# Reordering the first item of a fused block-sorted attention and gated MoE kernel, and issuing the later items' attention steps in pairs

## The chip, the cores and the metric

The kernel runs on one core of one Trainium2 chip. The metric is the device time of one execution in microseconds. Each comparison runs the kernel before and the variant in turn on the same chip, and a run of a single core is called slow when it is more than 1.5% above the fastest of the same kernel. Beside the time, each run records the length of its span and the mean clock that was granted to TensorE, as a share of full speed.

Four moments serve throughout as milestones, all read from TensorE's timeline: the **first scores** (first matmul into s_ps), the **second half of item 0** (the 33rd h matmul, the first for the second half of that item's tokens), the first h matmul of items 1, 2 and 3, and the end of TensorE. Everything ahead of the second half of item 0 is called the **front**.

## The reference

```python
for _ in range(5):                        # sinkhorn on (4, 8, 8, 8)
    P = exp(P - max(P, -1)); P = P / (sum(P, -1) + 1e-9); P = P / (sum(P, -2) + 1e-9)
k_sorted = einsum('bhij,bhjcd->bhicd', P, k_b)    # 8 blocks of 96 tokens, head_dim 64
v_sorted = einsum('bhij,bhjcd->bhicd', P, v_b)
attn = softmax(q_b @ k_sorted_b.T / 8)            # block i of q against sorted block i
x = (attn @ v_sorted_b) -> (3072, 512)            # batch 4, 8 heads, 768 tokens
out = maximum(x @ w1, x @ w2) @ w_out             # d_ff 1024
```

The kernel uses relu(x(w1 - w2)) + x w2 for the maximum, and multiplies w2 by w_out beforehand, so h is one product of 128x384 tiles and the output sums two.

## The kernel before

The four batch items follow one another. Item b's matmuls of h and of the output run while item b+1's attention steps are put between them. Only item 0's attention has nothing to hide behind. Dense zero matmuls, the fills, keep TensorE running while the sinkhorn iterations wait for VectorE.

```python
load_v(0, 0, 3); load_k(0); load_q(0)             # then weights, in order
...
keep_streaming(ps_f32("fill_ps"), 76 * 160, most=160)
for it in range(5):
    sinkhorn(it)            # at it 3 and 4: 3072 columns of fills behind the exponent
    ...                     # ScalarE turns the values in pieces
SC, VA, TR = att(0)         # steps: 8 scores, 8 values, 4 transpositions of x
sort_k(0, 0, 2048, "A"); sort_k(0, 1, 256, "D"); sort_k(0, 2, 256, "A")   # fills ahead of each
sort_v(0, 0, 0, "D"); sort_v(0, 1, 0, "A")
q_transposes(0, 0, "D")     # two head pairs
sort_v(0, 2, 0, "A"); scores(0, 0); sort_v(0, 3, 0, "D"); scores(0, 1)
q_transposes(0, 1, "D"); values(0, 0); ...
```

The letters say which engine empties the PSUM tile: A is ScalarE, D is VectorE. The kernel keeps four PSUM tiles of 128x1024 fp32.

The softmax here doesn't subtract the row's maximum and nothing guards it: scores larger than these inputs give would overflow.

Of the kernel before, what the change touches and what calls it, by code (L numbers as in the profile page):

```python
# [16 lines left out]
def kernel(  # L17
# [97 lines left out]
    kT = {}  # L115
# [62 lines left out]
    make_identity(nc, ident)  # L178
    load_k(0)
    load_q(0)  # L180
    load_w_columns(w2_sb, moe_w2, 0, 2)
    load_w_columns(w1_sb, moe_w1, 0, 1)
    load_w_columns(w1_sb, moe_w1, 1, 2)
# [3 lines left out]
    load_v(1)  # L187
# [12 lines left out]
    w_difference(0, nc.gpsimd)  # L200
    load_k(1)
# [24 lines left out]
    def sinkhorn(it):  # L226
        nc.scalar.activation(out=p_sb, in_=p_sb, func=AF.Exp)
        if it >= 3:
            late_zeros(it)
            keep_streaming(ps_f32("fill_ps"), 3072, it)  # L230
        nc.vector.reduce_sum(out=rowsum, in_=p_sb, axis=AX.X)
        nc.vector.reciprocal(out=rowsum, in_=rowsum)
        nc.vector.tensor_tensor(
            out=p_sb, in0=p_sb, in1=rowsum.to_broadcast([G, NB, NB]), op=ALU.mult
        )
        nc.vector.reduce_sum(out=colsum, in_=p_sb.transpose([0, 2, 1]), axis=AX.X)
        nc.vector.reciprocal(out=colsum, in_=colsum)
        nc.vector.tensor_tensor(
            out=p_bf if it == 4 else p_sb,
            in0=p_sb,  # L240
            in1=colsum.to_broadcast([G, NB, NB]).transpose([0, 2, 1]),
            op=ALU.mult,
        )
# [42 lines left out]
    def block_diagonals(b):  # L286

        pe = ps_f32("pe")
        kinds = [1] if b % 2 else [1, 0]
        for m in kinds:  # L290
            sel = (
                sel_k[b].rearrange("g h w -> g (h w)")
                if m
                else sel_v[b].rearrange("g h j -> g (h j)")
            )
            nc.tensor.matmul(
                pe[:, m * 64 : m * 64 + 64],
                sel,
                p_bf.rearrange("p i j -> p (i j)"),
                start=True,  # L300
                stop=True,
            )
        for m in kinds:
            pm = const.tile([128, NB, NB], FP32, tag=f"pm{m}", name="pm")
            nc.vector.tensor_tensor(
                out=pm,
                in0=pe[:, m * 64 : m * 64 + 64].rearrange("p (i j) -> p i j", j=NB),
                in1=maskJ[:, m].to_broadcast([128, NB, NB]).transpose([0, 2, 1]),
                op=ALU.mult,
            )  # L310
            pt = const.tile([128, NB], FP32, tag=f"pt{m}", name="pt")
            nc.vector.reduce_sum(out=pt, in_=pm, axis=AX.X)
            bd = const.tile([128, 8, NB], BF16, tag=f"bd{m}{b}", name="bd")
            nc.vector.tensor_tensor(
                out=bd,
                in0=maskM[:, m].to_broadcast([128, 8, NB]),
                in1=pt.to_broadcast([128, NB, 8]).transpose([0, 2, 1]),
                op=ALU.mult,
            )
            if m:  # L320
                bd_k[b] = bd.rearrange("p m i -> p (m i)")
            else:
                bd_v[b] = bd_v[b + 1] = bd.rearrange("p m i -> p (m i)")
# [18 lines left out]
    def q_transposes(b, half, eng=None):  # L342

        if half == 0:
            qT[b] = qpool.tile([128, HP, R, 128], BF16, tag="qT", name="qT")
        if b > 1:
            hps = slice(half * 2, half * 2 + 2)
# [6 lines left out]
        for n in range(2 * R):  # L354
            hp, r = half * 2 + n // R, n % R
            c = slice(n * 128, (n + 1) * 128)
            for h2 in range(2):
                nc.tensor.matmul(  # L358
                    ps[h2 * 64 : h2 * 64 + 64, c],
                    q_raw[b][:, hp + 4 * h2, r * D : (r + 1) * D],  # L360
# [6 lines left out]
            qT[b][:, half * 2 : half * 2 + 2].rearrange("p h r c -> p (h r c)"),  # L367
            ps[:, 0 : 2 * R * 128],
            2 * R * 128,
# [4 lines left out]
    def sort_k(b, t, n=0, eng=None):  # L374
# [4 lines left out]
        for c in range(16):  # L379
# [10 lines left out]
        evac(  # L390
            kT[b][:, 0 : 32 * BLK]
            .rearrange("p (m ch c) -> p ch m c", ch=2, m=32)[:, :, :, t * 16 : (t + 1) * 16],
            ps.rearrange("p (c ch m) -> p ch m c", ch=2, m=32),
            1024,
            eng=eng,
        )

    def sort_v(b, t, n=0, eng=None):
# [3 lines left out]
        for m in range(16):  # L402
# [10 lines left out]
            ps[0:BLK].rearrange("p (d m) -> p m d", m=64),  # L413
            1024,
# [246 lines left out]
    keep_streaming(ps_f32("fill_ps"), 76 * 160, most=160)  # L661
    for it in range(5):
        sinkhorn(it)
# [4 lines left out]
        if it == 2:  # L668
            selections(0)
            turn_v(first, "A", 0, 18)  # L670
        if it == 3:
            turn_v(first, "A", 18, 36)
    turn_v(first, "A", 36, 56)
    turn_v(first, "A", 56, 80)
    block_diagonals(0)
    turn_v(first, "D", 80, 96)

    SC, VA, TR = att(0)
    sort_k(0, 0, 2048, "A")
    sort_k(0, 1, 256, "D")  # L680
    sort_k(0, 2, 256, "A")
    sort_v(0, 0, 0, "D")
    sort_v(0, 1, 0, "A")
    q_transposes(0, 0, "D")
    sort_v(0, 2, 0, "A")
    scores(0, 0)
    sort_v(0, 3, 0, "D")
    scores(0, 1)
    q_transposes(0, 1, "D")
    values(0, 0)  # L690
# [3 lines left out]
    values(0, 2, 256)  # L694
    x_transposes(0, 0, "A")
    VA[3]()
    SC[4]()
    moe_h_products(0, 0, 0, (0, 2), 256)
    x_transposes(0, 1, "A")
    w_difference(1)  # L700
    moe_h_products(0, 0, 1, (0, 2))
    for b in range(1, B):
        selections(b)
    w_difference(2)
    w2_out = w2_transposes(0, "D")
    moe_h(0, 0, 0, "A", (1, 3))
    w2_out()
    w_difference(3)
    moe_h(0, 0, 1, "A", (1, 3))
    SC[5]()  # L710
# [5 lines left out]
    def load_rest():  # L716
# [4 lines left out]
        0: [VA[4]],  # L721
        1: [SC[6], SC[7], VA[5]],
        2: [VA[6], TR[2], VA[7]],
        3: [TR[3], lambda: w2_transposes(1, "A")(), load_rest, lambda: block_diagonals(1)],
# [8 lines left out]
    for b in range(B):  # L733
# [15 lines left out]
        if b == B - 1:  # L749
            units += [  # L750
                lambda: moe_out_last(4, [(0, 512, "D")]),
                lambda: moe_out_last(5, [(0, 256, "A"), (256, 384, "D"), (384, 512, "A")]),
            ]
        steps, lo = [], 2
        if b < B - 1:
            qs = [lambda half=half: q_transposes(b + 1, half) for half in range(2)]
# [6 lines left out]
            if b == 0:  # L763
                lo = 9
                tail[7] += ks
# [3 lines left out]
                steps = group(*vs[:3]) + qs[:1] + group(*SC[0:2], vs[3]) + qs[1:] + VA[:1]  # L769
                steps += group(*SC[2:5]) + VA[1:2]  # L770
            elif b == 1:
                vs = [lambda t=t: sort_v_pair(2, t) for t in range(8)]
                tail[1] = qs
                tail[10] = [lambda: pair_q(3, 0), lambda: pair_q(3, 1)]
                steps = group(*ks) + group(*vs[0:3]) + group(*vs[3:6]) + group(*vs[6:8])
                steps += group(*SC[0:2]) + group(*SC[2:4]) + VA[:2]
            else:
                tail[1] = qs
                tail[4] = ks
                steps = group(*SC[0:2]) + group(*SC[2:5]) + VA[:2]  # L780
                lo = 6
            rest = SC[4:] if b == 1 else SC[5:]
            steps += VA[2:3] + TR[:1] + VA[3:4]
            steps += group(*rest[:-1]) + TR[1:2] + VA[4:5] + rest[-1:] + VA[5:6]
            steps += TR[2:3] + VA[6:7]
# [10 lines left out]
        tail = {0: [VA[7], TR[3]]}  # L796
# [28 lines left out]
```

## Time and profile before

| | value |
|---|---|
| median (range) of the first three runs | 178.76 us (177.56 to 180.59) |
| profiled span, clock | 175.0 us, 0.998 |
| first scores | 18.53 us |
| second half of item 0 | 35.66 us |
| first h of items 1, 2, 3 | 74.22, 110.55, 144.31 us |
| end of TensorE, of the span | 171.6, 175.0 us |

These lines are of the kernel before. On the page below, each digit of a row is the busy share, or the clock, of one of 40 equal slices in tenths; a queue row gives packets, MB and share.

```profile
span 175.0 us, 4519 instructions
...
PEclk9999999999999999999999999999999999999999
...
q8 instruction: 16, 0.26, 0.6%
```

The row of queue 8 is easily skipped. It says that a DMA queue moved 16 packets of instructions, 0.26 MB or 16 KB each, while the kernel ran. TensorE's timeline: start, busy time, operation, count, and in brackets the idle time before it with what ended it. In all these lines PE is TensorE, PEld its weight loads, DVE VectorE, ACT ScalarE and POOL GpSimd; L82 is a line of the kernel.

```profile
9.43 2.54 PE L82 MATMUL fill_ps<-fill,late 128*128 128x512 bf16 x11
...
12.05 1.04 PE L82 MATMUL k_ps<-fill 128*128 128x512 bf16 x4
...
13.65 0.28 PE L82 MATMUL k_ps<-fill 128*128 128x256 bf16 x1
```

Fills stand in every gap from 1.2 to 14.5 us, and no bracket appears between them.

### The profile page before, as it was taken

Reading aid. Unit: us, or ns where it says so; the run is one execution under the profiler, and the core shown is the slowest. Engines: PE = TensorE matmul, PEld = TensorE weight load, DVE = VectorE, ACT = ScalarE, POOL = GpSimd, SP = SyncE. Lnnn points to the kernel's source line nnn. Section 1 sums busy time; section 2 is a strip of 40 time slices with the busy share of each in tenths; the row PEclk is TensorE's granted clock in tenths of the full one; section 3 lists DMA queues with packets and bytes.
Section 4 is the critical chain, followed back from the end, with each engine's and each line's share of the span. In section 5 each row is a group of like instructions: output and inputs, shape, how many; then the busy total and the mean of one; then the engine's idle time right before and its main releaser. Section 6 shows DMA issues by size and latency. Waiting matters only on the chain.

```text
span 175.0 us, 4519 instructions
## 1 busy us (share of the span) xinstructions
PE 162.3 (93%) x1999; PEld 99.8 (57%) x2014; DVE 83.1 (47%) x186; ACT 79.9 (46%) x98; POOL 22.9 (13%) x39
## 2 busy tenths in 40 slices
PE   7999799999999899997999899999798999899992
PEld 7948666756665454466665445566454446454461
DVE  5867797559355737225638324235254442221110
ACT  4576576797253454069880622436803106330030
POOL 7951453122302002000000000000000000000000
PEclk9999999999999999999999999999999999999999
DMA  4999999999999952999201245292024154400333
GB/s 59 200 206 204 202 209 214 206 202 208 220 209 205 196 151 51 117 245 270 64 0 22 87 104 156 104 208 48 0 48 140 27 165 142 26 0 0 120 123 120
DMA packets 29811, 23.11 MB, mean 132 GB/s; under 512 B 16672, under 2 KB 24736, under 8 KB 29792
## 3 DMA queue, kind: packets, MB, share of 16 engines
q0 software_dynamic: 10304, 12.58, 42.5%
q1 hardware_dynamic: 19200, 10.04, 23.6%
q8 instruction: 16, 0.26, 0.6%
q10 hardware_dynamic: 288, 0.20, 0.3%
q14 instruction: 3, 0.02, 0.0%
HBM read 25.17 MB, written 6.29 MB: 180 GB/s over the span
## 4 chain that ended last, share of the span: by engine, by line
PE 73%; DMA 9%; ACT 6%; issue 5%; DVE 2%; POOL 2%; ACTq 0%; DVEq 0%; POOLq 0%
PE out_ps L612 33%; PE h_ps L585 23%; DMA q_raw<-in_q_dram 7%; PE wc_ps L563 4%; PE o_ps L477 3%; PE k_ps L383 3%; ACT e L458 3%; PE s_ps L450 2%; DMA xT<-x 2%; ACT g L599 2%; PE tq_ps L358 1%; PE v_ps L404 1%; DVE qT L106 1%; PE tw_ps L540 1%; POOL k_raw L145 1%
## 5 line engine op out<-in xcount | busy, mean ns | idle before, releaser
L612 PE MATMUL out_ps<-wo_sb,g 128*128 128x512 bf16 (+2 forms) x198 | 46.2, 362 | 1.8 <-DVE o L106 0.7
L585 PE MATMUL h_ps<-xT,w_sb 128*128 128x384 bf16 x256 | 45.2, 326 | 1.9 <-DMA xT<-x 0.8
L585 PEld LDWEIGHTS <-w_sb 128*128 128x128 bf16 x256 | 24.1, 98 | 17.4 <-issue 2.3
L458 ACT ACTIVATE e<-s_ps 96x768 bf16<-96x768 f32 x32 | 24.0, 807 | 19.4 <-PE s_ps L450 19.4
L612 PEld LDWEIGHTS <-g 128*128 128x128 bf16 x208 | 18.0, 97 | 17.5 <-issue 1.2
L599 ACT ACTIVATE g<-h_ps 128x768 bf16<-128x768 f32 x23 | 18.6, 812 | 18.1 <-PE h_ps L585 18.1
L612 PE MATMUL out_ps<-wc,xT 128*128 128x512 bf16 (+2 forms) x103 | 24.8, 362 | 0.1
L104 ACT COPY o<-out_ps 128x1024 f32<-128x1024 f32 x8 | 8.1, 1012 | 35.7 <-PE out_ps L612 29.4
L494 DVE TENSOR_TENSOR x<-o_ps,rs 96x512 bf16<-96x512 f32 x32 | 22.0, 687 | 1.1
L488 DVE RECIPROCAL rs<-o_ps 96x8 f32<-96x8 f32 x32 | 6.4, 201 | 32.2 <-PE o_ps L477 32.2
L601 DVE TENSOR_SCALAR g<-h_ps 128x768 bf16<-128x768 f32 x9 | 8.6, 957 | 18.2 <-PE h_ps L585 18.2
L612 PEld LDWEIGHTS <-xT 128*128 128x128 bf16 x104 | 9.9, 98 | 10.9
L477 PEld LDWEIGHTS <-e 96*128 96x128 bf16 x256 | 11.7, 97 | 7.0 <-issue 0.9
L477 PE MATMUL o_ps<-v_sb,e 96*128 96x65 bf16 x256 | 13.1, 193 | 1.4 <-ACT e L458 1.0
L106 DVE CAST v_sb<-v_ps 96x1024 bf16<-96x1024 f32 x8 | 9.7, 1217 | 8.0 <-PE v_ps L425 5.1
L450 PE MATMUL s_ps<-qT,kT 64*128 64x96 bf16 x256 | 9.2, 204 | 1.6 <-DVE qT L106 0.9
L104 ACT CAST kT<-k_ps 128x1024 bf16<-128x1024 f32 x9 | 8.8, 1016 | 3.0 <-PE k_ps L383 3.0
L450 PEld LDWEIGHTS <-kT 64*128 64x128 bf16 x256 | 6.3, 94 | 6.6 <-issue 4.8
L104 ACT CAST v_sb<-v_ps 96x1024 bf16<-96x1024 f32 x8 | 7.9, 1012 | 3.8 <-PE v_ps L404 3.7
L82 PEld LDWEIGHTS <-fill 128*128 128x128 bf16 x84 | 8.7, 123 | 1.7 <-DVE fill L73 1.2
L82 PE MATMUL fill_ps<-fill 128*128 128x160 bf16 x76 | 8.2, 292 | 1.2 <-DVE fill L73 1.2
L106 DVE COPY o<-out_ps 128x1024 f32<-128x1024 f32 x3 | 3.7, 1225 | 9.3 <-PE out_ps L612 9.3
(73 smaller groups left out, 132.5 us busy)
## 6 DMA issues: line engine op xcount, KB each, us to landing
out_dram<-o SPq DMA_DIRECT2D x11, 512.0 KB, 3.0
k_raw<-in_k_dram POOLq DMA_DIRECT2D x12, 256.0 KB, 12.4
q_raw<-in_q_dram POOLq DMA_DIRECT2D x4, 768.0 KB, 10.8
v_raw<-in_v_dram POOLq DMA_DIRECT2D x6, 384.0 KB, 12.7
w_sb<-in_moe_w_dram POOLq DMA_DIRECT2D x3, 512.0 KB, 16.0
wo_sb<-in_moe_w_out_dram POOLq DMA_DIRECT2D x2, 512.0 KB, 19.9
v_raw<-in_v_dram POOLq DMA_DIRECT2D x3, 256.0 KB, 4.6
w_sb<-in_moe_w_dram POOLq DMA_DIRECT2D x2, 256.0 KB, 14.1
```

The source lines that it names most:

```text
L82: nc.tensor.matmul(ps[:, 0:w], w0, fill[:, 0:w], start=True, stop=True)
L104: nc.scalar.copy(out=out_ap, in_=in_ap)
L106: nc.vector.tensor_copy(out=out_ap, in_=in_ap)
L450: nc.tensor.matmul(ps[:, h2 * 512 + ii * 128 : h2 * 512 + ii * 128 + BLK], kT[b][rows, (hp * 8 + i) * BLK : (hp * 8 + i) * BLK + 128], rhs ...
L458: nc.scalar.activation(out=e[:, 0 : 8 * BLK].rearrange("p (t c r) -> p t c r", t=8, r=R), in_=ps[0:BLK] .rearrange("p (t f) -> p t f", t=8 ...
L477: nc.tensor.matmul(ps[:, h2 * 512 + ii * 65 : h2 * 512 + (ii + 1) * 65], e[:, (h2 * 4 + ii) * BLK : (h2 * 4 + ii) * BLK + 128], v_sb[:, m0 ...
L494: nc.vector.tensor_tensor(out=x, in0=ov[:, :, :, 0:D], in1=rs.to_broadcast([BLK, 2, 4, D]), op=ALU.mult,)
L563: nc.tensor.matmul(wc_ps[0][:, m * 512 : (m + 1) * 512], w2T[:, fb, dmt * 128 : (dmt + 1) * 128], wo_sb[:, fb, :], start=(fb == 0), stop=( ...
L585: nc.tensor.matmul(h_ps[t][:, m * 512 : m * 512 + TCH], w1_sb[:, hp, fb * 128 : (fb + 1) * 128], xT[:, b % 2, ch, hp % 2, hp // 2, :], sta ...
L599: nc.scalar.activation(out=g, in_=src, func=AF.Relu)
L601: nc.vector.tensor_scalar(out=g, in0=src, scalar1=0.0, scalar2=None, op0=ALU.max)
L612: nc.tensor.matmul(dst, g_tiles[b, ch, m // 2][:, m % 2, off : off + 128] if m < NFB else xT[:, b % 2, ch, hp % 2, hp // 2, off : off + 12 ...
```

## The change

The intent: let the scores start from one head pair of queries, let values of the first four blocks be ready early, take the fills out where real work can stand, and issue the later attention steps in pairs so that four PSUM tiles have time to empty.

```diff
+    load_q(0)
     load_k(0)
-    load_q(0)
-    load_w_columns(w2_sb, moe_w2, 0, 2)
-    load_w_columns(w1_sb, moe_w1, 0, 1)
-    load_w_columns(w1_sb, moe_w1, 1, 2)
+    for w in range(2):
+        load_w_columns(w2_sb, moe_w2, w, w + 1)
+        load_w_columns(w1_sb, moe_w1, w, w + 1)
...
-    def sinkhorn(it):
+    def sinkhorn(it, meanwhile=None):
         nc.scalar.activation(out=p_sb, in_=p_sb, func=AF.Exp)
-        if it >= 3:
+        if meanwhile:
+            meanwhile()                     # VectorE turns 11 columns of values
+        if it == 4:
             late_zeros(it)
-            keep_streaming(ps_f32("fill_ps"), 3072, it)
+            keep_streaming(ps_f32("fill_ps"), 2048, it)
...
-    keep_streaming(ps_f32("fill_ps"), 76 * 160, most=160)
+    keep_streaming(ps_f32("fill_ps"), 174 * 72, most=72)
...
-    sort_k(0, 0, 2048, "A")
-    sort_k(0, 1, 256, "D")
-    sort_k(0, 2, 256, "A")
-    sort_v(0, 0, 0, "D")
-    sort_v(0, 1, 0, "A")
-    q_transposes(0, 0, "D")
-    sort_v(0, 2, 0, "A")
-    scores(0, 0)
+    q_transposes(0, 0, 1, "A")              # one head pair
+    sort_v_half(0, 0, 0, "D")               # first four blocks, 32 columns
+    sort_v_half(0, 0, 1, "A")
+    sort_k(0, 0, 0, "D")
+    sort_k(0, 1, 0, "A")
+    sort_k(0, 2, 0, "AD")                   # emptied in two halves
+    SC[0]()
... (item 0's remaining steps, with the second half sorts between values 1 to 3)
-                lambda: moe_out_last(5, [(0, 256, "A"), (256, 384, "D"), (384, 512, "A")]),
+                lambda: moe_out_last(5, [(0, 384, "D"), (384, 512, "A")]),
...
-            steps += VA[2:3] + TR[:1] + VA[3:4]
-            steps += group(*rest[:-1]) + TR[1:2] + VA[4:5] + rest[-1:] + VA[5:6]
-            steps += TR[2:3] + VA[6:7]
+            steps += group(*SC[0:2]) + VA[0:1] + group(*SC[2:4]) + VA[1:2] + group(VA[2], TR[0])
+            steps += group(*SC[4:6]) + VA[3:4] + group(VA[4], TR[1]) + group(*SC[6:8]) + VA[5:6]
+            steps += group(VA[6], TR[2]) + VA[7:8] + TR[3:4]
...
-        tail = {0: [VA[7], TR[3]]}
+        tail = {}
```

## The prediction

The spacing of 31 ns in its later stages is that of 48 value matmuls in 1.50 us, at 46.73 us of the trace before, and the 0.17 us of a free array are the author's estimate from it and from the page's mean of 193 ns (L477). Its rate of 205 GB/s is from the GB/s row of the profile's page (207 from 4.4 to 61 us). That VectorE works off its queue in the order of the program was assumed for the walk; the waits for x (1.14, 1.46 and 1.56 us, walked as 1.2, 1.7 and 1.7) agree with it.

> **What bounds the kernel now.** I read the page first, then the chain of waits in order of time, then the timeline of each engine with the idle time in brackets.
>
> ```profile
> PE 162.3 (93%) x1999; PEld 99.8 (57%) x2014; DVE 83.1 (47%) x186; ACT 79.9 (46%) x98; POOL 22.9 (13%) x39
> ```
>
> TensorE is the bound on average, the other engines are half empty. So only two things can shorten the kernel: fewer TensorE instructions on the path, or less time in which TensorE stands still. The chain says where it starts, and the timeline where it stands still:
>
> ```profile
> 5.09 11.48 DMA q_raw<-in_q_dram
> 16.57 0.04 issue
> 16.61 0.88 PE tq_ps L358 x24
> ```
> ```profile
> 18.53 0.35 PE L450 MATMUL s_ps<-qT,kT 64*128 64x96 bf16 x8 [0.48 <-DVE qT L106]
> ...
> 20.63 0.40 PE L477 MATMUL o_ps<-v_sb,e 96*128 96x65 bf16 x8 [0.35 <-DVE v_sb L106]
> ...
> 57.57 0.40 PE L477 MATMUL o_ps<-v_sb,e 96*128 96x65 bf16 x8 [0.62 <-ACT e L458]
> ...
> 81.30 0.41 PE L425 MATMUL v_ps<-bd,v_dc 64*128 64x64 bf16 x16 [0.51 <-ACT kT L104]
> ...
> 82.22 1.46 PE L585 MATMUL h_ps<-xT,w_sb 128*128 128x384 bf16 x8 [0.51 <-ACT kT L104]
> ...
> 99.08 1.89 PE L612 MATMUL out_ps<-wo_sb,g 128*128 128x512 bf16 x7 [0.53 <-ACT o L104]
> ...
> 123.39 0.35 PE L450 MATMUL s_ps<-qT,kT 64*128 64x96 bf16 x8 [0.35 <-ACT e L458]
> ...
> 124.09 1.46 PE L585 MATMUL h_ps<-xT,w_sb 128*128 128x384 bf16 x8 [0.35 <-ACT e L458]
> ...
> 132.84 1.89 PE L612 MATMUL out_ps<-wo_sb,g 128*128 128x512 bf16 x7 [0.68 <-DVE o L106]
> ...
> 151.01 5.04 PE L585 MATMUL h_ps<-xT,w_sb 128*128 128x384 bf16 x30 [0.76 <-DMA xT<-x]
> ```
>
> The reader is to see three regions. Until 16.6 us the inputs arrive (values, keys, queries, in that order, and the queries last). From 18.5 to about 35 us the first item's attention runs with little other work beside it. After that TensorE is nearly full, and its stops are short waits for a PSUM tile that ScalarE or VectorE has not emptied yet (three score tiles issued in a row, three key tiles and three value tiles in a row), and one wait for a transpose by DMA.
>
> [...] 12 matmuls of 512 columns took 2.59 us, 216 ns each. [...] the page's GB/s row stays near 205 for the first 60 us whatever is asked, so changing the order of loads moves landings but not the last one.
>
> **The change part by part.**
>
> *Loads.* Queries now come before keys. The three inputs are the same bytes, so the last of them (now the third key chunk) lands where the queries landed, 16.57 us. The queries land at about 16.6 minus three key chunks of 1.3 us (the queue's waits for k_raw ended at 9.3, 10.65 and 11.9), that is 12.7.
>
> *Sinkhorn.* One iteration took 1.44 us of VectorE plus 0.3 for the exponent. The VectorE turns of 11 columns (352 words; 512 took 0.60 and 768 took 0.83, so about 0.45) overlap the exponent but are longer than that gap, and the selections move to iteration 1. I get p_bf at 12.0 instead of 11.3. That is no loss: keys land later than that anyway. The fill is 174x72 against 76x160 columns, about as long, and ends near 9.6.
>
> *First scores.* Key tile 3 is multiplied at 16.6 to 17.3 (0.69 as before). Its eviction is split between ScalarE (0.59, estimated from 1.01 for 1024 and 0.37 for 256) and VectorE (0.69, as the 512-column output copy). But in the built program the VectorE half waits for the ScalarE half, so it is 1.3 us in series: scores start at **18.7** against 18.53. Nothing gained.
>
> *From the first score to the second half of item 0.* Here I walked the built order by hand with the durations of before: scores 0.25 of TensorE and 0.35 to the result, exponent 0.81 (0.70 back to back), values 0.25/0.40, reciprocal and product 0.87, eviction of 1024 1.01 on ScalarE and 1.22 on VectorE, xT copy 0.80, relu 0.81/0.96, w2T copy 1.22. The half value sorts are 32 matmuls at 25 to 30 ns (0.8 to 1.0 us) where a quarter was 16 (0.5), so four cost 1.3 us more in all, two of them after the first score. The steps that bind:
> - values 0 at 20.3 (before 20.63), values 1 at 21.4, values 2 at 23.1, values 3 at 24.2 (before 23.57).
> - VectorE has the eviction of the last value half at 24.4 to 25.6 ahead of product 3, which ends at 26.5: TensorE waits 1.2 us for it with the second x transpose.
> - Its xT copy ends at 27.8: TensorE waits 0.8 with the second half of h 0.
> - From 30.3 VectorE holds, in order, relu of h 1, product 4, the w2T copy, product 5, a weight difference, product 6, an xT copy, a difference, four selections, product 7: 7.6 us in a row. Transpose 2 needs product 5 (34.05) and waits 1.7; transpose 3 needs product 7 (37.9) and waits 1.7.
> - The h products of the second half start at about 40.6; before they start at 35.7.
> Saved fills (3 of 256 columns, 0.3 us) are in that sum. **Front: +4.9 us.**
>
> *Later stages.* The brackets from 50 us on (0.33, 0.62, 0.51, 0.51, 0.53, 0.28, 0.35, 0.35, 0.68, 0.76 and two of 0.16) sum to 5.2; each is counted from the last result, while the array was free 0.17 earlier (a matmul of 193 ns at a spacing of 31), 2.0 more: 7.2 us. Scores in pairs, with an output or h unit between, leave four PSUM tiles time to empty, and the last transpose is issued two units before the item's end instead of after the next begins, so most go. New ones that I find in the built order: value tiles right behind three key tiles in item 0 (0.6) and a second score behind a value tile (0.45), the h unit after the keys in item 1 (0.6), small ones (0.9): 2.5. **Later: -4.7 us.**
>
> *Tail.* The last tile in two pieces (384 and 128) has the same columns as three. The 192 KB piece leaves 0.1 us after the last matmul and its DMA needs about 3.3 (128 KB took 3.0, 256 KB 3.7), where before the last 64 KB piece left 0.3 after and needed 2.1. **+0.6 us** (estimate, 0.5 to 1).
>
> Sum: +4.9 - 4.7 + 0.6 = +0.8 us.
>
> **The rivals.** *The front is not lost.* If ScalarE or VectorE run a little ahead of my walk, the waits for products 3, 5 and 7 shrink: each is a chain of five or six short steps. Against it: VectorE's order is fixed, and 7.6 us of work stand between relu 1 and product 7. If half of the loss goes, the time is about 176.5. *The gain of the pairs is lost to PSUM.* Four tiles are few, one is held by the running output, and the key and value evictions remain at 1 to 1.2 us; if the stops only move, later gain is 2 us and the time 182. *TensorE work as the bound.* If only instruction counts mattered, there would be 0.8 us more of small value matmuls and 1.5 us fewer fills, and nothing would be seen: 178. *The DMA order.* The first difference of weights for h 1 moved to GpSimd (2.1 us each) ahead of the next values' load; these loads then start near 24 us, while the queue still holds about 1.5 MB of weights, 7 us at 205 GB/s, so I count nothing.
>
> **Range and chances.** The median before is 178.76, over 177.56 to 180.59, so about 1% is noise. The two large terms, each near 5 us with opposite signs, are each uncertain by about 2; with the noise that gives some 3 us either way. I take 178.6, a little under the sum of 179.6, because an order as deliberate as this was probably looked at on a chip, which tells for the first rival. Faster by over 2% means under 175.2: 0.18. Slower means over 182.3: 0.12. Within 2%: 0.70.
>
> **What would show it.** Right: the first score near 18.7 with the VectorE half of the key eviction after the ScalarE half; TensorE idle on x before the second, third and fourth transposes of item 0, over 4 us together; h of the second half near 40; after that no bracket over 0.6, and none on xT at the last item; the last DMA a 384-column one. Wrong: second half of h before 37 us would mean that I overstated VectorE's queue; brackets of 0.5 at each pair would mean that PSUM still limits.

## The result and the profile after

The changed kernel takes **185.72 us** in the median of four runs (185.03 to 186.35), the kernel before 178.16 in the same rounds. The ratio is 1.0448, with a 95% interval from 1.0361 to 1.0535. Ratios here are the mean time of one kernel's fast runs over that of the other's of the same rounds, so they are not quite the ratio of the medians. The prediction had taken 178.6 us, and gave a time over 182.3 a chance of 0.12.

| milestone, us | before | predicted | after |
|---|---|---|---|
| first scores | 18.53 | 18.7 | 21.65 |
| second half of item 0 | 35.66 | 40.6 | 46.89 |
| from there to the first h of item 1 | 38.56 | | 38.96 |
| item 1 to 2, 2 to 3 | 36.33, 33.76 | | 35.09, 33.18 |
| item 3 to the end of TensorE | 27.33 | | 26.13 |
| tail | 3.39 | +0.6 | 3.04 |
| from the second half of item 0 to the end | 139.37 | -4.1 | 136.40 (-2.97) |
| granted clock | 0.998 | | 0.952 |

So the front costs 11.2 us instead of 4.9. The lines of the page that answer to those of before:

```profile
span 183.3 us, 4786 instructions
...
PEclk9985569699999999999999999999999999999999
...
q8 instruction: 17, 0.28, 0.6%
```

PEclk is 8, 5, 5 and 6 in the third to sixth slice and 6 in the eighth, where it was 9: TensorE ran at half speed for part of the front. One more packet of instructions was fetched, and TensorE has 2,148 matmuls, each with a weight load, in place of 2,014 (the trace holds the record of each load; of the matmuls 18 and 15 records are missing). The next lines are a table by stage of the changed kernel, cut every 3.41 us: the granted clock of this trace changes at 12.17, 25.82, 32.65, 36.06 and 182.84 us, which lie whole multiples of 3.41 us apart. Its columns are the length, the busy time of TensorE, its weight loads, VectorE, ScalarE and GpSimd, each with the number of its instructions, then the clock, the DMA share and GB/s.

```profile
8.76:12.17 3.41, 0.96 (x8) 0.42 (x6) 3.07 (x16) 2.39 (x4) 0.60 (x1) 1.00 1.28 210
12.17:15.58 3.41, 2.86 (x79) 2.49 (x78) 2.39 (x9) 0.80 (x1) 1.48 (x2) 0.50 1.16 204
...
18.99:22.41 3.42, 1.02 (x17) 0.74 (x18) 0.69 (x1) 0.80 (x2) 2.41 (x2) 0.50 1.34 203
...
29.24:32.65 3.41, 1.67 (x22) 0.96 (x21) 1.60 (x3) 1.17 (x2) 0.54 (x1) 1.00 1.20 225
32.65:36.06 3.41, 3.41 (x19) 1.46 (x17) 0.00 (x0) 1.84 (x3) 1.06 (x2) 0.50 1.03 201
```

From 8.76 to 12.17 us TensorE was busy for 0.96 us of 3.41, because the fills ended at 8.9 and the next came at 11.17. In the window after that the clock is 0.50, and it stays there for four windows. A second sparse window, 1.67 us at 29.24, costs another. In the kernel before, the window from 10.35 to 13.77 us was busy throughout. The changed kernel's timeline of TensorE shows the rest:

```profile
11.17 0.81 PE L82 MATMUL fill_ps<-fill,late 128*128 128x512 bf16 x3 [2.26 <-DVE rowsum L234]
...
15.58 2.72 PE L385 MATMUL k_ps<-bd,k_raw 64*64 64x64 bf16 x94
19.99 0.26 PE L385 MATMUL k_ps<-bd,k_raw 64*64 64x64 bf16 x2 [1.69 <-issue]
21.65 0.50 PE L478 MATMUL s_ps<-qT,kT 64*128 64x96 bf16 x8 [1.41 <-DVE kT L106]
...
30.93 0.51 PE L543 MATMUL tx_ps<-ident,x 96*128 96x96 bf16 x8 [1.14 <-DVE x L522]
...
33.85 2.54 PE L613 MATMUL h_ps<-xT,w_sb 128*128 128x384 bf16 x8
...
40.25 0.51 PE L543 MATMUL tx_ps<-ident,x 96*128 96x96 bf16 x8 [1.46 <-DVE x L522]
...
44.12 0.51 PE L543 MATMUL tx_ps<-ident,x 96*128 96x96 bf16 x8 [1.56 <-DVE x L522]
```

Four things are to be read. The fill at 11.17 waited 2.26 us. Of the 96 key matmuls 94 were issued without a break, then TensorE stood still for 1.69 us and no engine is named as the cause ("issue"), then came the last two. The three waits for x are those that the prediction walked (1.2, 1.7 and 1.7). And eight h matmuls took 2.54 us where they take 1.47 at full clock. The two halves of the third key tile, from the timelines of ScalarE and VectorE:

```profile
20.29 0.59 ACT L104 CAST kT<-k_ps 128x512 bf16<-128x512 f32 x1 [1.74 <-PE k_ps L385]
20.90 0.69 DVE L106 CAST kT<-k_ps 128x512 bf16<-128x512 f32 x1 [3.00 <-ACT kT L104]
```

They ran in series, as predicted, VectorE's behind ScalarE's.

The trace puts one packet of the instruction queue, 16,384 bytes, at 17.64 us, taking 974 ns. That is while TensorE was in the third key tile, and the DMA row has its highest digit (90% or more) in every slice from 12 to 18 us. The counts of the two pages go with TensorE's instructions (each matmul and its weight load): 16 packets at 4,028 in the kernel before, 17 at 4,296 in the changed one, so 252 and 253 to a packet. So queue 8 is read as TensorE's instruction stream; the places where the experiments stood still (below, at e12 and e13) agree with that. The rival to that reading was that TensorE's waits for VectorE and for PSUM explain the whole front, with the clock and the wait as side effects. The working theory became: **the front lost about 5 us as walked, and the rest to a late instruction fetch and to the halved clock.**

### The profile page after: what moved, and what is told of

Read it like the earlier page. It is cut to its first block, busy times and chain, and to the rows that moved or that the text cites. A ratio compares the mean times of both kernels' runs of the same rounds, so it can differ in the third digit from the quotient of the medians.

```text
span 183.3 us, 4786 instructions
## 1 busy us (share of the span) xinstructions
PE 164.7 (90%) x2130; PEld 101.7 (56%) x2148; DVE 85.9 (47%) x191; ACT 78.6 (43%) x95; POOL 26.0 (14%) x41
## 4 chain that ended last, share of the span: by engine, by line
PE 77%; DVE 8%; DMA 5%; ACT 3%; issue 3%; POOL 1%; DVEq 0%; ACTq 0%; POOLq 0%
PE out_ps L640 33%; PE h_ps L613 23%; DMA q_raw<-in_q_dram 5%; PE s_ps L478 4%; PE wc_ps L591 4%; PE o_ps L505 4%; PE k_ps L385 3%; ACT kT L104 2%; DVE x L522 2%; PE tq_ps L360 2%; PE v_ps L430 1%; DVE v_sb L106 1%; DVE g L629 1%; PE v_ps L410 1%; PE v_ps L453 1%
## 5 line engine op out<-in xcount | busy, mean ns | idle before, releaser
L613 PE MATMUL h_ps<-xT,w_sb 128*128 128x384 bf16 x256 | 46.2, 333 | 1.6 <-ACT xT L104 0.6
L629 DVE TENSOR_SCALAR g<-h_ps 128x768 bf16<-128x768 f32 x11 | 10.5, 958 | 31.5 <-PE h_ps L613 31.5
L627 ACT ACTIVATE g<-h_ps 128x768 bf16<-128x768 f32 x21 | 17.0, 810 | 19.0 <-PE h_ps L613 19.0
L104 ACT COPY o<-out_ps 128x1024 f32<-128x1024 f32 x9 | 9.1, 1012 | 26.2 <-PE out_ps L640 24.6
L640 PEld LDWEIGHTS <-xT 128*128 128x128 bf16 x100 | 9.6, 97 | 11.2
L106 DVE CAST kT<-k_ps 128x1024 bf16<-128x1024 f32 (+1 forms) x6 | 6.7, 1134 | 14.6 <-PE k_ps L385 11.6
L106 DVE CAST v_sb<-v_ps 96x1024 bf16<-96x1024 f32 x9 | 11.0, 1218 | 5.5 <-PE v_ps L410 3.6
L385 PE MATMUL k_ps<-bd,k_raw 64*64 64x64 bf16 x384 | 8.1, 204 | 1.7 <-issue 1.7
L385 PEld LDWEIGHTS <-k_raw 64*64 64x64 bf16 x384 | 7.5, 120 | 2.9 <-issue 2.8
L82 PE MATMUL fill_ps<-fill 128*128 128x72 bf16 x174 | 7.7, 220 | 1.2 <-DVE fill L73 1.2
L106 DVE COPY o<-out_ps 128x1024 f32<-128x1024 f32 x2 | 2.4, 1224 | 12.8 <-PE out_ps L640 9.5
```

What stands on the lines that cost most here:

```text
L82: nc.tensor.matmul(ps[:, 0:w], w0, fill[:, 0:w], start=True, stop=True)
L104: nc.scalar.copy(out=out_ap, in_=in_ap)
L106: nc.vector.tensor_copy(out=out_ap, in_=in_ap)
L385: nc.tensor.matmul(ps[r0 : r0 + 64, m * 64 : (m + 1) * 64], kv[r0 : r0 + 64, t * 16 + m, :], bd_k[b][r0 : r0 + 64, :], start=True, stop=True,)
L613: nc.tensor.matmul(h_ps[t][:, m * 512 : m * 512 + TCH], w1_sb[:, hp, fb * 128 : (fb + 1) * 128], xT[:, b % 2, ch, hp % 2, hp // 2, :], sta ...
L627: nc.scalar.activation(out=g, in_=src, func=AF.Relu)
```

## The experiments

All 15 kernels gave correct results. The kernel before ran in the same rounds each time, at 178.17 us (e1 to e4), 177.92 (e6 to e9), 178.56 (e5, e10 to e12) and 177.42 (e13 to e15).

| kernel | median us (lowest to highest) | profiled clock | first scores | second half of item 0 | from there to the end |
|---|---|---|---|---|---|
| e1 long late fills | 184.82 (182.67 to 186.15) | 0.991 | 21.11 | 44.64 | 136.0 |
| e2 87 fills | 183.18 (182.93 to 185.31) | 0.962 | 19.66 | 44.55 | 136.4 |
| e3 both | 183.39 (181.15 to 184.29) | 0.979 | 19.03 | 43.09 | 136.0 |
| e4 pairs only | 173.14 (173.10 to 173.25) | 1.000 | 18.52 | 35.66 | 135.8 |
| e5 front only | 188.21 (186.78 to 188.25) | 0.954 | 21.33 | 46.65 | 138.0 |
| e6 fills in two more gaps | 183.12 (179.37 to 184.76) | 0.980 | 22.57 | 45.50 | 136.0 |
| e7 less on VectorE | 181.94 (179.42 to 183.26) | 0.981 | 23.52 | 45.01 | 136.1 |
| e8 key tile whole | 183.65 (179.54 to 186.16) | 0.944 | 22.07 | 48.75 | 135.4 |
| e9 pairs, q by head pair | 173.15 (172.52 to 174.66) | 1.000 | 17.69 | 35.86 | 135.4 |
| e10 loads held | 182.99 (182.44 to 183.36) | 0.962 | 19.84 | 43.76 | 136.4 |
| e11 values whole | 183.33 (179.07 to 185.68) | 0.981 | 18.41 | 43.15 | 136.1 |
| e12 = e3 again | 184.03 (one run) | 0.972 | 20.64 | 45.94 | 136.0 |
| e13 = changed kernel again | 186.59 (one run) | 0.933 | 21.66 | 48.07 | 136.4 |
| e14 held and warm | 183.32 (182.09 to 185.10) | 0.961 | 20.02 | 45.98 | 136.0 |
| e15 = e9, loads held | 177.42 (176.31 to 178.55) | 0.990 | 17.44 | 39.13 | 135.2 |

The medians are of all runs, slow ones among them: one each of e1 and e14, two each of e3, e7 and e11, three each of e6 and e8; the profiled runs of e6, e7 and e8 are slow ones. The last column is nearly constant where the later steps are the same. So the columns before it say where the time of each variant was decided.

### e1, e2, e3: the fills

e1 puts the late fills back, e2 makes half as many fills of twice the width, e3 does both.

```diff
-        if it == 4:
+        if it >= 3:                                                  # e1, e3
             late_zeros(it)
-            keep_streaming(ps_f32("fill_ps"), 2048, it)
+            keep_streaming(ps_f32("fill_ps"), 3072, it)
...
-    keep_streaming(ps_f32("fill_ps"), 174 * 72, most=72)
+    keep_streaming(ps_f32("fill_ps"), 87 * 144, most=144)             # e2, e3
```

> The changed kernel with the two fills of 3072 columns of the kernel before put back into Sinkhorn iterations 3 and 4 (12 more PE matmuls, nothing else). Theory 'clock': TensorE idled from 8.7 to 11.2 us, so its clock was halved from 12.2 to 25.8 us; with the fills the granted clock is 1.0 there, the value halves and key tiles run at the speed of before, and the time falls by 2 to 4.5 us (185.7 to about 182). Theory 'instructions' (TensorE waited 1.7 us at 18.3 us inside the third key tile for its own instructions, which come by DMA): that stop stays, since no instructions were taken away, and the first score stays near 21.6 us. Rival (clock costs nothing because the inputs arrive late anyway): under 1 us.

> The changed kernel with its first fill as 87 matmuls of 144 columns instead of 174 of 72: the same columns, 174 PE instructions fewer ahead of the first item. Theory 'instructions': the stop of 1.7 us inside the third key tile goes or moves to a sparser place, the first score comes at about 20 us instead of 21.65, and the time falls by 1 to 2 us; the clock is still halved from about 12 us. Rival (the stop is a late key chunk or another wait on data): the first score stays at 21.6 and the time does not change.

> Both edits. If my walk in the prediction failed only in these two things, the granted clock is near 1.0, the first score is at 18.7 to 19.3 us, the second half of item 0's h at about 41 us, and the time falls by about 6 us to 179.5. Rival (the losses overlap: each hides the other or the later stages take the gain back): less than 4.5 us, with no addition of e1 and e2.

e1 adds 8 fills, not the 12 of its expectation, since the changed kernel had kept 4. In e1 the clock stayed full until 20.74 us, then was half for one window. The halved clock up to there is thus made by the missing fills. The standing still in the key sort remained (2.07 us), and the window that held it was the one that halved the clock. In e2 that wait was 0.23 us, and the first scores came 2.0 us earlier than in the changed kernel, while the clock was half from 11.08 to 17.90 and from 28.14 to 34.97. In e3 both were mended as far as the first scores: 19.03 us, near the predicted 18.7. Yet the second half of item 0 was still at 43.09, and the clock was half from 24.94 to 31.76. The table by stage of e3 shows why that is not an idle gap:

```profile
21.53:24.94 3.41, 3.17 (x101) 2.98 (x102) 2.41 (x6) 3.32 (x5) 2.83 (x3) 1.00 1.24 206
24.94:28.35 3.41, 2.93 (x28) 1.66 (x26) 1.99 (x3) 0.53 (x2) 2.59 (x6) 0.50 1.24 206
```

The window ahead of the halving counts TensorE busy for 3.17 of 3.41 us. It held 101 matmuls of 32 to 96 columns over 64 or 96 rows: scores, values, half sorts, one transposition. So the busy time that the profile counts does not decide it; a sum of work parts the windows that were read. Take the 96 windows of 3.41 us at full clock in the traces of the kernel before and of the changed one, and sum from the records each window's matmuls as columns times rows/128. The four that a half one followed have 1,408 (changed, at 179.42 us), 1,536 (changed, at 8.76, and before, at 170.78) and 2,496 (changed, at 29.24). The 92 others have at least 3,448 (before, at 20.60). This window of e3 has about 3,000, an estimate from the merged lines of its timeline. By busy time they do not part: the clock stayed full after a window busy for 1.77 us (e2, at 38.38, about 3,460 by the same estimate; the next eight h matmuls took 1.47 us), and here it did not after 3.17. That is read from the records; no run varied it alone. All three remain 3.2 to 3.5% slower than the kernel before (fast runs alone; one run of e1 and two of e3 are slow), so each part brought little by itself. By its time e1 is the rival's case: 0.9 us below the changed kernel, though of another session, where 2 to 4.5 were expected. e2 is 2.5 us below it, more than expected, and e3 misses the 179.5 us of its expectation even in its fastest run (181.15).

### e4: the pairs alone

The kernel before with the new order of the later items, the last output tile in two pieces, and the old loads, sinkhorn and item 0.

```diff
-            steps += VA[2:3] + TR[:1] + VA[3:4]
-            steps += group(*rest[:-1]) + TR[1:2] + VA[4:5] + rest[-1:] + VA[5:6]
-            steps += TR[2:3] + VA[6:7]
+            steps += group(*SC[0:2]) + VA[0:1] + group(*SC[2:4]) + VA[1:2] + group(VA[2], TR[0])
+            steps += group(*SC[4:6]) + VA[3:4] + group(VA[4], TR[1]) + group(*SC[6:8]) + VA[5:6]
+            steps += group(VA[6], TR[2]) + VA[7:8] + TR[3:4]
... (with lo, ks, vs, qs and tail as in the changed kernel)
```

> The opposite part: loads, Sinkhorn, first item and its tail as before the change; only the later items' steps in pairs and the last tile in two pieces. Theory (the later stages gained 2.6 us in the two traces: -0.4, 1.2, 0.6 and 1.2 by item; the loss is all in the front): 2 to 3.5 us faster than before, about 175.5. Rival (the later stages gain only because they start later, with all loads long landed): under 1 us.

It takes **173.14 us**, ratio 0.9732 (0.9689 to 0.9774): faster than both kernels. The front is that of before to 0.01 us, and everything after it is 3.6 us shorter (135.8 against 139.37). All four runs had a clock of 0.998 to 1.0. Beside that, three of the six fast runs of before in these rounds have a clock of 0.99 and spans of 176.4 to 176.7 us, where the two at 1.0 have 175.1 and 175.2; so the medians differ by 5.0 us and the profiled spans by 3.5. Where those runs of before lose their clock was not traced. The brackets of over 0.2 us after 50 us in e4 are two, where the prediction counted ten in the kernel before (just ahead of that, at 49.64, stands one of 0.56 us without a releaser):

```profile
81.79 1.46 PE L610 MATMUL h_ps<-xT,w_sb 128*128 128x384 bf16 x8 [0.51 <-ACT kT L104]
...
122.65 1.46 PE L610 MATMUL h_ps<-xT,w_sb 128*128 128x384 bf16 x8 [0.36 <-DVE g L626]
```

### e5: the front alone

The changed kernel with the later steps of before.

```diff
-                steps = group(*ks) + group(*vs[0:2]) + group(vs[2], qs[0]) + group(vs[3], qs[1])
+                steps = group(*vs[:3]) + qs[:1] + group(*SC[0:2], vs[3]) + qs[1:] + VA[:1]
+                steps += group(*SC[2:5]) + VA[1:2]
... (likewise for the other items)
```

> The new front (loads in the order values, queries, keys; half sorts; queries by head pair; turn of values in the gaps; small fills) with the old single steps of the later items. Theory (front and pairs are two independent terms: pairs alone gave 173.14 against 178.17, that is -5.0, and both together 185.72 against 178.16, that is +7.6): front alone costs +12.6, about 190.5 us, with the second half of item 0's h at 45 to 48 us. Rival (the pairs lose in the new front, since item 0 ends with work that item 1's steps used to cover): front alone costs only 7 to 9 us, 185 to 187 us.

It takes 188.21 us, 9.65 more than the kernel before (178.56) and 2.5 more than the changed kernel's 185.72 of another session. Both expectations miss: the terms do not simply add to 190.5, and the pairs are not worthless in the new front. Part of the difference is that in the fast profiles of e4 the pairs save 3.6 us after the front, in the changed kernel against e5 1.6 (136.4 against 138.0); e5 keeps the new two-piece tail, 0.35 us of it, and its four runs are all at 0.936 to 0.954 of the clock. What remains of the 3 us was not taken apart.

### e6, e7, e8: what is left in item 0

e6 adds fills to e3 ahead of the first scores and of the second transposition.

```diff
-    SC[0]()
+    scores(0, 0, 3072)
...
     moe_h_products(0, 0, 0, (0, 2))
+    keep_streaming(ps_f32("fill_ps"), 2048)
     x_transposes(0, 1, "A")
```

> The kernel with small second fills and long late fills (e3), and beside them fills of TensorE in the two remaining empty stretches: 3072 ns ahead of the first scores and 2048 ns ahead of the second transposition of values. Clock theory: what is left of the halved clock in the front (24.94 to 31.76 us in e3) goes, the clock is 1.0 or nearly so throughout, the second half of item 0's h begins at 40.6 to 41.3 us (43.09 in e3), and the time falls by 2 to 2.5 us to about 181. Rival (the queue of VectorE sets these stages, the clock is beside the point): the clock goes up, h begins where it did within 0.5 us, and the time stays within 0.7 us of e3.

In three of four runs the expectation failed. (They are called slow, being over 1.5% above the fourth; their mean clock was 0.979 to 0.981 where the fourth had 1.0, and one core alone was at work.) In the profiled one TensorE stood still for 2.30 us in the second key tile, a wait which e3 had not shown; the clock was half from 17.07 to 23.90; and the fills ahead of the scores, now too late, held TensorE until 22.57. But the one run at a clock of 1.0 took **179.37 us** (span 177.3). With 136.0 from the second half of item 0 to the end, that puts its second half at 41.3 us (an estimate by difference), against 40.6 in the prediction's walk.

e7 moves three pieces of work of item 0 from VectorE to ScalarE on top of e6.

```diff
-    sort_v_half(0, 1, 1, "D")
+    sort_v_half(0, 1, 1, "A")
...
-    moe_h(0, 0, 1, "D")
+    moe_h(0, 0, 1, "A")
...
-    w2_transposes(0, "D")()
+    w2_transposes(0, "A")()
```

> e6 with three pieces of work of the front moved from VectorE to ScalarE: the eviction of the last half of sorted values, the relu of the first gate halves, and the copy of the transposed second weight. Theory (VectorE's queue in item 0 is what the x transpositions wait for, 0.7, 0.7, 1.6 and 1.7 us in e3): these waits shrink to 1.5 us in sum and h's second half begins 3 us earlier than in e6. Rival (ScalarE becomes the queue): the waits change name to ScalarE and keep their sum within 1 us, and the time is within 1 us of e6.

TensorE's waits for x, from the view of waits between 18 and 46 us, in e6 and then in e7 (total, times, longest):

```profile
PE tx_ps L543 <- DVE x L522: 3.3, 3, 1.6
```
```profile
PE tx_ps L543 <- DVE x L522: 1.9, 2, 1.5
```

From the first scores to the second half of item 0 it took 21.5 us instead of 22.9. So VectorE's queue is what TensorE waits for there, and half of the wait can be moved away; the last of them, before the transposition that needs product 7, hardly shrank. The gain is half of what was expected, and the times do not tell the two apart (fast runs 179.42 and 180.75 us in e7, 179.37 in e6).

e8 is e3 with the third key tile emptied whole by ScalarE.

```diff
-    sort_k(0, 2, 0, "AD")
+    sort_k(0, 2, 0, "A")
```

> e3 with the third tile of sorted keys evicted whole by ScalarE instead of in two halves by ScalarE and VectorE. Theory (the two halves ran one after the other, 0.59 and 0.69 us[...]): one whole eviction of about 1.0 us starts the first scores 0.3 us earlier (18.7 in place of 19.03 us), and the time changes by less than 0.5 us. Rival (halves are side by side on the chip and the order of the trace misleads): the first scores begin 0.3 to 0.4 us later than in e3.

The time says nothing here: its runs span 179.54 to 186.16 us for another reason. TensorE's program is that of e3, yet its timeline has these lines:

```profile
19.32 1.59 PE L385 MATMUL k_ps<-bd,k_raw 64*64 64x64 bf16 x51 [3.39 <-issue]
22.07 0.50 PE L478 MATMUL s_ps<-qT,kT 64*128 64x96 bf16 x8 [1.17 <-ACT kT L104]
```

From the last key matmul to the scores the wait is 1.17 us in place of 1.41, 0.24 less, about what was expected. And 3.39 us were lost before, in a program that lost none of it in e3.

### e9: queries by head pair in the old front

e4 with the queries turned one pair at a time.

```diff
-    q_transposes(0, 0, 2, "D")
+    q_transposes(0, 0, 1, "D")
     sort_v(0, 2, 0, "A")
     scores(0, 0)
+    q_transposes(0, 1, 1, "D")
     sort_v(0, 3, 0, "D")
     scores(0, 1)
-    q_transposes(0, 2, 2, "D")
+    q_transposes(0, 2, 1, "D")
+    q_transposes(0, 3, 1, "D")
```

> The later steps in pairs on the old front (e4, 173.14 us), with the queries turned by head pair in the old front as the one part of the new front that moves no load. Theory (only the first pair's turn and eviction stands ahead of the first scores): first scores at 17.75 us against 18.52, and a time 0.3 to 0.8 us below e4, 172.3 to 172.8. Rival (the first scores wait for the third key tile, so q is beside the point): first scores at 18.5 us, time within 0.3 us of e4.

The first scores came at 17.69 us, as expected, and nothing came of it: the second half of item 0 began at 35.86, 0.20 later than in e4, and the time is 173.15. The 0.83 us won at the first scores stand against a wait of 0.90 us without a releaser in the fourth scores:

```profile
22.67 0.22 PE L475 MATMUL s_ps<-qT,kT 64*128 64x96 bf16 x2 [0.90 <-issue]
```

Whether the 0.83 would have lasted without it, this run does not tell. Against the kernel before the ratio is 0.9748 (0.9678 to 0.9818): faster, but whether by 2% is unclear.

### e10: the loads held back

The changed kernel, with the loads of the weights and of item 1 issued only when item 0's last keys have landed.

```diff
-    for w in range(2):
-        load_w_columns(w2_sb, moe_w2, w, w + 1)
-        ... (all weights, w_difference 0 and 1, load_v(1), load_k(1))
...
     block_diagonals(0)
+    gate = const.tile([128, 1], BF16, tag="gate", name="gate")
+    nc.gpsimd.tensor_copy(out=gate, in_=k_raw[0][:, HB * D - 1 : HB * D])
+    ... (the same loads and differences, in the same order)
```

> The changed kernel with the loads of the weights and of item 1 held back until item 0's last keys have landed (some 17 us), so that the DMA engines are quiet while the third key tile is sorted. Theory (TensorE's 1.69 us of standing still inside that tile is an instruction fetch that waits behind the loads): no wait of over 0.7 us without a releaser inside the key sort, last key matmul by 18.6 us. Rival (the wait is something else, the loads are beside the point): it is there as before, 1.5 us or longer. The time is not what this asks: h may wait for weights that now land some 5 us later.

The wait is gone: all 96 key matmuls were issued in a row. First the timeline, then the busy share of the DMA engines from 12 to 18 us in 40 slices of 0.15 us, of e10:

```profile
15.60 2.77 PE L375 MATMUL k_ps<-bd,k_raw 64*64 64x64 bf16 x96
```
```profile
DMA  9999999999999999999653104000000000000000
```

The same slices of the changed kernel:

```profile
DMA  9999999999999999999999999999999999999999
```

In e10 the loads thin out from 15 us on, and the instruction packet starts at 15.66. In the changed kernel the DMA engines stay full, and with the same number of TensorE instructions ahead of it the packet starts at 17.64. That is the experiment on the cause: it changed no TensorE instruction, and the wait of 1.69 us went. The first scores came 1.8 us earlier, and the medians, though of different sessions, are 182.99 against 185.72 with the kernel before at 178.56 and 178.16. The weights came late enough to be feared and were in time.

### e11: values sorted whole

e3 with item 0's values sorted in four tiles of 16 columns, as in the kernel before.

```diff
-    sort_v_half(0, 0, 0, "D")
-    sort_v_half(0, 0, 1, "A")
+    sort_v(0, 0, 0, "D")
+    sort_v(0, 1, 0, "A")
...
+    sort_v(0, 2, 0, "A")
     SC[0]()
+    sort_v(0, 3, 0, "D")
... (and without the two later half sorts)
```

> e3 (small second fills and long late fills) with item 0's values sorted whole, four tiles of 16 columns around the first scores as in the kernel before, in place of the sort by half of the blocks. Theory (the second half sort and its two evictions of 1.1 to 1.2 us stand in the queues of VectorE and ScalarE between values and transpositions): the later x waits fall by 1.5 to 3 us and h's second half begins 1.5 to 3 us earlier after the first scores than in e3 (24.06 us there), while the first scores come 0.3 to 0.6 us later. Rival (the waits belong to the order of scores, values and transpositions): from first scores to h's second half stays within 0.7 us of 24.06.

The rival has it: from the first scores to the second half of item 0 it took 24.74 us, 0.7 more than in e3, and the waits for x came to 4.0 us in place of 3.4. So the sort by half of the blocks is not what makes item 0 long. That leaves the order of scores, values and transpositions, which no run changed by itself. Contrary to the expectation the first scores came 0.6 us earlier, since the last keys landed earlier here: the third key tile, which waits for them in both traces, began at 16.31 us and in e3 at 16.94.

### e12, e13: two kernels again

No edit: e12 is e3, e13 is the changed kernel, each once more on another chip.

> e3 once more, unchanged. If the late fetch is fixed by the program: first scores at 19.0 us again and no wait of over 1 us in the key sort. If it is a chance of the run: a wait of 1.5 to 3.5 us may stand in the second key tile, as in e8, whose TensorE program is the same, and the fetch starts at 16 to 17 us instead of 12.70.

> The changed kernel once more, unchanged. If fixed by the program: 1.7 us of standing still after the 94th key matmul (as also in e5, 1.53 us, whose front is the same), first scores at 21.3 to 21.7 us, half clock from 12 to 26 us again. If a chance of the run: another place or length of the wait, first scores 0.7 us or more away.

e12 stood still as e8 did, and e13 as the changed kernel did, in the same places, with 51 and with 2 of the 96 key matmuls still to come; these lines of TensorE's timeline are of e12 and of e13:

```profile
17.81 1.38 PE L385 MATMUL k_ps<-bd,k_raw 64*64 64x64 bf16 x51 [2.11 <-issue]
```
```profile
20.00 0.26 PE L385 MATMUL k_ps<-bd,k_raw 64*64 64x64 bf16 x2 [1.80 <-issue]
```

So the **place** is fixed by the program, and the other traces show to the matmul how. e1 has 8 matmuls more ahead of it than the changed kernel and stood still 8 earlier, behind the 86th. e2 has 87 fewer, which would make the 181st; it stood still behind the 53rd, 128 earlier. e3 with both would come to the 173rd, and with 128 taken off to the 45th, where e6, e7, e8, e12 and e14 did stand still. 128 matmuls with their weight loads are 256 instructions, about the 252 to 253 that the two pages give to a packet. So the places repeat packet by packet (an inference from these traces). These lines are of e1 and of e2:

```profile
19.36 0.34 PE L385 MATMUL k_ps<-bd,k_raw 64*64 64x64 bf16 x10 [2.07 <-issue]
```
```profile
16.85 1.27 PE L385 MATMUL k_ps<-bd,k_raw 64*64 64x64 bf16 x43 [0.23 <-issue]
```

The **length** depends on when the packet comes. Set side by side, with the packet's start and length from the trace:

| kernel | after key matmul | packet starts, takes | TensorE goes on at | after the packet's end | stood still |
|---|---|---|---|---|---|
| changed | 94 | 17.64, 0.97 | 19.99 | 1.38 | 1.69 |
| e13 (same) | 94 | 17.58, 0.98 | 20.00 | 1.44 | 1.80 |
| e5 (same front) | 94 | 17.48, 0.97 | 19.66 | 1.21 | 1.53 |
| e10 (loads held) | (94) | 15.66, 0.96 | | | none |
| e1 | 86 | 17.10, 0.89 | 19.36 | 1.37 | 2.07 |
| e2 | 53 | 14.63, 0.95 | 16.85 | 1.27 | 0.23 |
| e3 | (45) | 12.70, 0.94 | | | none |
| e12 (= e3) | 45 | 15.36, 0.94 | 17.81 | 1.51 | 2.11 |
| e8 (TensorE as e3) | 45 | 16.87, 0.95 | 19.32 | 1.50 | 3.39 |
| e6 | 45 | 16.16, 0.97 | 18.37 | 1.24 | 2.30 |
| e7 | 45 | 17.04, 0.89 | 19.32 | 1.39 | 3.22 |
| e14 (below) | 45 | 14.94, 0.89 | 17.21 | 1.38 | 1.48 |

In every trace that shows the wait TensorE goes on 1.2 to 1.5 us after the packet has ended. Why the packet came at 12.70 us in e3 and at 15.36 in e12, of the same program, these runs do not tell; in e3 the DMA engines stood at 8 to 9 tenths from 13 us on, and e12 ran on another chip. So a single trace such as e10's could owe something to chance; but the three traces of the changed front agree on their packet within 0.16 us, and e10's came 1.8 us before the earliest of them. The clock's loss is not fixed by the program either: e13's clock was half from 13.05 to 36.95 us, where the changed kernel's was for 17.1 us in two stretches, and its second half of item 0 began 1.18 us later.

### e14: both causes at once

e10 with e3's fills and with e6's fills ahead of the second transposition.

> Both causes taken away at once: the loads of weights held back as in e10, the second fills 87 of 144 columns, 3072 ns of late fills in the last two iterations, and 2048 ns of fills ahead of the second transposition. Theory (beyond the walked +5.0 us the front loses to late fetches and the halved clock alone): no wait without a releaser of over 0.7 us in the key sort, clock 0.99 to 1.0, first scores at 18.8 to 19.3 us, h's second half at 40.6 to 41.5 us, and 178.5 to 180 us in all runs. Rival (there is a third loss): the same clock and fetches, and h's second half later than 42.3 us, or runs above 181 us at a full clock.

The theory's numbers were not met: 183.32 us, clock 0.961, second half of item 0 at 45.98. But its conditions were not met either. With 87 fills TensorE is through its 45th key matmul at 15.7 us, and the loads of item 0 itself, which cannot be held back, thin out only from 14.7 us on; the packet came at 14.94 and the wait, again behind the 45th key matmul, was 1.48 us:

```profile
17.21 1.28 PE L375 MATMUL k_ps<-bd,k_raw 64*64 64x64 bf16 x51 [1.48 <-issue]
```

The clock was half from 17.69 to 24.52 and from 38.17 to 45.00 us. So the two causes could not be taken away together by these means, and a front with nearly the full clock was seen only in single runs: 179.37 (e6, clock 1.0), 179.42 (e7, 0.99), 179.54 (e8, 0.99) and 179.07 (e11, 0.99). No trace of such a run exists.

### e15: loads held in the best version

e9 with its weights' loads held back in the same way, behind its queries.

> e9 (pairs, queries by head pair, old front) with the weights' loads held back until its queries have landed. Theory (a late fetch cost e9 0.90 us in the third scores): that wait goes, and the time falls by 0 to 0.9 us, to 172.2 to 173.1. Rival (here the weights are needed at 24.6 us and come too late): h waits for its weights and the time rises by 1 us or more.

Here the rival holds: 177.42 us, 4.3 more than e9 (of another session) and the same as the kernel before (177.42). The wait that was asked about did go: all eight matmuls of the fourth scores were issued in a row, and the packet came at 16.77 us where e9's came at 20.23. So in a second kernel, by one trace of each, such a wait went when the loads were held back. But the first h matmuls waited:

```profile
26.05 1.46 PE L601 MATMUL h_ps<-xT,w_sb 128*128 128x384 bf16 x4 [2.07 <-POOL w_sb L184]
```

The difference of weights on GpSimd, which needs the late weights, is what they wait for; in that gap the clock fell for one window (25.75 to 29.16 us). The best version stays e4, or e9 with it: 173.1 us.

## Why the prediction was wrong

**The mechanism that was walked is right.** The loads land as walked (queries used from 12.98 us against 12.7, last keys by 16.92 against 16.57), the halves of the key tile run in series (0.59 and 0.69 us), and the waits for x behind VectorE's queue are 1.14, 1.46 and 1.56 us against 1.2, 1.7 and 1.7. e7 showed that they are VectorE's. The one run at full clock puts the front's cost at some 5.6 us (41.3 against 35.66, an estimate by difference), against +4.9.

**The step that failed is the front's sum "+4.9", by what it left out.** Of the later end of sinkhorn the prediction said "That is no loss: keys land later than that anyway". It let TensorE stand idle from the end of the fills (9.6 us by its walk, 8.9 in the trace) without a cost, and counted the removed fills only as columns. Two costs follow. First, taking out the fills left TensorE busy for 0.96 us in one window of 3.41, and the clock was then half for 13.65 and later for another 3.41 us; e1 showed that the fills keep the clock full up to 20.74 us. Second, with 174 small fills and 64 more sorting matmuls a fetch of instructions falls into the key sort while the loads fill the DMA engines: 1.69 us. e10 showed the cause by moving the loads alone. By the estimate of 5.6 us these two, with what follows from them, make some 5.6 of the 11.2 us, and the walk itself missed about 0.7. The 1.69 is measured; the clock's share is by difference, since no trace of the new front has both taken away. Two traces that nearly part them fit: e10, without the wait but at half clock for 13.65 us, began the second half of item 0 3.1 us before the changed kernel, and e1, with a wait of 2.07 us but one half window, 2.25 us before it.

**The later stages' term was mis-sized.** It read -4.7 and measured -2.6 (2.97 less 0.35 of the tail), or -3.2 in the old front (e4). The waits went as said: the brackets after 50 us sum to 1.96 us (0.29, 0.24, 0.51, 0.43, 0.49) in the changed kernel where they were 4.92 (5.2 with two of 0.16 us that stand where a matmul's record is missing; the changed kernel has four of these). That is 2.96 less, near what was measured. But 2.0 us more had been counted for the array being free ahead of each bracket, and that gain did not appear.

**The tail had the wrong sign.** Predicted +0.6, measured -0.35: the 192 KB piece took 1.9 us from issue to landing and the last 64 KB piece 1.7, where the prediction had taken 3.3 for the former from the kernel before, in which four pieces were in flight close together. In the changed kernel three were; whether that is why each landed sooner was not tested. The last DMA was the 128-column piece, not the 384-column one that the prediction named as a sign.

**The discount was wrong too.** The text took a number under its own sum because so deliberate an order "was probably looked at on a chip". No view of the profile said so.

The rivals named none of this. The one that came nearest, "TensorE work as the bound", counted the fills as plain saved time.

## What to carry to other kernels

Fills in a gap are not idle work: before you take one out, read the granted clock window by window, and count TensorE's work behind a sparse window at half speed (here, behind a window busy for 1.67 of 3.41 us, the clock was 0.50 and eight h matmuls took 2.54 us in place of 1.47). Small matmuls cost instruction fetches as well as time (17 packets for 4,296 instructions here, 16 for 4,028), and a fetch that fell where the loads fill the DMA engines stopped TensorE here for 0.2 to 3.4 us, so split wide fills only if you must. When a change has independent parts, run each alone: here the pairs alone gave -2.7%, hidden under a front that lost more.
